# A spatial mix in seven half-size products instead of eight, in a fused attention and MLP kernel on one Trainium2 core

## The chip, the core and the metric

The kernel is one program on one core of a Trainium2 chip. The core has TensorE for matmuls (PE in the rows; PEld is its weight load), VectorE (DVE), ScalarE (ACT), GpSimd (POOL) and SyncE (SP, which here only issues transfers). Each engine works through its own instructions in order and waits on semaphores where it needs another's result. Matmul results land in PSUM, which TensorE writes and VectorE and ScalarE read; everything else lies in SBUF. The metric is the device time of one execution in microseconds (us). Lower is better.

## The reference, cut to what matters

Three parts follow one another: a hash-masked attention, a channel mix (`_moe_ref`) and a gated MLP with a mix along the sequence (`_moe2_ref`). The change lies in the last:

```python
def _moe2_ref(x, w_in, w_spatial, b_spatial, w_out):      # x (2, 768, 512)
    h = np.maximum(x @ w_in, 0.0)                         # (2, 768, 1024)
    u, v = (h[..., :512], h[..., 512:])
    mu = np.mean(v, axis=-1, keepdims=True)
    var = np.mean((v - mu) ** 2, axis=-1, keepdims=True)
    v_n = (v - mu) / np.sqrt(var + 1e-06)
    v_s = np.einsum('ts,bsd->btd', w_spatial, v_n) + b_spatial[None, :, None]
    gated = u * v_s
    return (gated @ w_out).astype(np.float32)
```

For each of the two batches the spatial mix is one product of a 768x768 matrix with a 768x512 matrix.

## The kernel before, in words

Every product is made three times at reduced precision to keep that of float32: each operand is held as a rounded high part and a remainder (low part), and `mm3` issues high by high, high by low and low by high (L178-184, so all its matmuls carry L183). A high part is a copy on ScalarE; the remainder is one subtraction of two SBUF tensors, on VectorE unless GpSimd is named (`split`, L129).

The order of the work is written out by hand. The steps are issued one after the other, and each ends with `tick()`, which issues the small jobs planned for that tick (`at_tick`, `later`). The last part has twelve token columns of 128 in three groups n of 512 tokens, and these steps:

- `step_u(n)`, four products of 12 matmuls: the half u of h, evacuated by a ReLU on ScalarE into XT (L772). It reads the group's input from `slots`, four tiles with high and low part; group 2 goes into the tiles that group 0 had, so `plan_split(2, ...)` fills them during the w steps (copy L650 on ScalarE, remainder L654 on VectorE).
- `step_w(n)`, four products of 12: the half v for 128 tokens each; here called a row. ReLU on ScalarE (L787), statistics and their aggregation on VectorE (L791, L792), then two ticks later a square root on ScalarE (L800), reciprocal and normalisation on VectorE (L801, L802), and a tick later the split into `vn`.
- `step_s(b, hf)`, four products of 18 matmuls with 384 columns: the spatial mix for one batch and one half of the output tokens. VectorE adds the bias (L826), multiplies with u (L828), and the result is split into a `parked` tile.
- `step_o(b, hf)`, three products of 12: the output product, copied by ScalarE (L851) and sent out by SP.

Their order is u0 u1 w0 w1 u2 w2, then s and o with the two batches interleaved. Transposed w_spatial is fetched by `plan_fetch` (once through SP, once rounded through GpSimd's queue) from tick 62 on, and its remainder is VectorE's (L757). The output weights' second half is prepared at ticks 78 and 81 by `plan_out`; the first row of w0 ends at tick 68, the last of w2 at 83. Products rotate through six PSUM banks (`bank`), so TensorE can be up to six products ahead of their readers.

Of the kernel before, what the change touches and what calls it, by code (L numbers as in the profile page):

```python
# [20 lines left out]
DM = 512  # L21
# [609 lines left out]
def mixers(tc, nc, mid, wide, top, XT, slots, parked, epsT, wr, wk, wv, w_in, w_spT, b_sp, w_out, out, split,  # L631
# [27 lines left out]
    with tc.tile_pool(name="m1", bufs=1) as m1:  # L659
# [62 lines left out]
        plan_out((2, 3), (78, 81))  # L722
# [14 lines left out]
    with tc.tile_pool(name="m2", bufs=1) as m2:  # L737
        vn, wsp = {}, []
        more = top.tile([128, 4, TB], F32, tag="x", name="more").bitcast(F32R).rearrange("p (m t) n -> p m t n", m=2)
        slots[6:] = [more[:, n] for n in range(2)]  # L740
# [3 lines left out]
        def plan_fetch(c, n):  # L744
            st = {}

            def load():
                t = mid.tile([128, 512, 2], U32, tag="w_raw", bufs=2, name="wst")
                st["t"] = t.rearrange("p a b -> p (a b)")[:, :S].bitcast(F32)
                nc.sync.dma_start(st["t"], w_spT[128 * c:128 * c + 128, :])  # L750
                if c % 3 == 0:
                    wsp.append(wide.tile([128, 2, 3, S], F32R, tag="PT", bufs=2, name="wsp"))
                nc.gpsimd.dma_start(wsp[c // 3][:, 0, c % 3, :], w_spT[128 * c:128 * c + 128, :])  # L753

            def rest():
                w = wsp[c // 3]
                nc.vector.tensor_sub(w[:, 1, c % 3, :], st["t"], w[:, 0, c % 3, :])  # L757

            at_tick(n, load)
            at_tick(n + 2, rest)  # L760
# [14 lines left out]
        def step_w(n):  # L775
            for j in range(4):
# [9 lines left out]
                t = m2.tile([128, DM], F32, tag="vt", bufs=4, name="vt")  # L786
# [6 lines left out]
                if n < 2:  # L793
                    tt = m2.tile([128, 2, DM], F32R, tag="vn", bufs=8, name="vn")
                else:
                    tt = wr[:, :, j, :]
                vn[divmod(4 * n + j, 6)] = tt

                def scale(t=t, mv=mv, sd=sd):
# [10 lines left out]
        def step_s(b, hf):  # L810
            t0 = hf * HS
            for m in range(4):
                o = bank("s")
                ms = slice(128 * m, 128 * m + 128)
                mm3(
                    o[:, :HS],
                    [
                        (
                            (vn[b, c][:, 0, ms], vn[b, c][:, 1, ms]),
                            (wsp[c // 3][:, 0, c % 3, t0:t0 + HS], wsp[c // 3][:, 1, c % 3, t0:t0 + HS]),  # L820
                        )
                        for c in range(6)
                    ],
                )
                f = mid.tile([128, HS], F32, tag="d", bufs=1, name="gs")
                nc.vector.tensor_add(f, o[:, :HS], bb[:, t0:t0 + HS])  # L826
                g = m2.tile([128, DM], F32, tag="vt", bufs=4, name="g")[:, :HS]
                nc.vector.tensor_mul(g, f, XT[:, m, b, t0:t0 + HS])  # L828
                t = parked[4 * hf + m]
                split(g, t[:, 0], t[:, 1])  # L830
                tick()

        def step_o(b, hf):
            for j in range(3):
# [5 lines left out]
                for cs in ((slice(0, 256), slice(256, DM)) if last else (slice(0, DM),)):  # L840
# [12 lines left out]
                    if last:  # L853
                        o = bank("o")
# [86 lines left out]
```

## Time and profile before

| | us |
|---|---|
| median of 3 runs (lowest, highest) | 532.88 (532.85, 533.25) |
| the profiled execution | 533.83 |
| its span, first to last instruction | 532.0 |

| engine | busy us | share of the span |
|---|---|---|
| TensorE | 526.0 | 99% |
| VectorE | 381.0 | 72% |
| ScalarE | 319.5 | 60% |
| GpSimd | 142.6 | 27% |

The rows below give a start in us from the span's start, a duration, the engine, the line of the program, the operation, what it writes and reads, and how many instructions were merged (x). Matmuls overlap, so their pace is read from start to start and not from a mean duration. In brackets stands the time the engine had been idle, and what ended it.

### The profile page before, as it was taken

What the parts mean: (1) busy time and instruction counts of PE and PEld (TensorE: products, weight loads), DVE (VectorE), ACT (ScalarE), POOL (GpSimd) and SP (SyncE); (2) the same over time, 40 slices, a digit from 0 to 9 for tenths busy, and PEclk for the clock granted to TensorE, in tenths of its full rate; (3) what the DMA queues carried; (4) which work ended last, traced back from release to release, by engine and by line L of the source; (5) the groups of instructions that cost most, each with busy time, mean ns of one, the idle gap of its engine ahead of it and who ended that gap; (6) DMA issues with size and microseconds to landing.
All of it is one profiled execution on the core that took longest, in us unless ns stands there. A gap on an engine that the chain in (4) does not pass through costs nothing.

```text
span 532.0 us, 8226 instructions
## 1 busy us (share of the span) xinstructions
PE 526.0 (99%) x2886; PEld 423.6 (80%) x2886; DVE 381.0 (72%) x794; ACT 319.5 (60%) x659; POOL 142.6 (27%) x157
## 2 busy tenths in 40 slices
PE   8999999999999999999999999999999999999997
PEld 6778676868687776688888888888888889989996
DVE  8787898888979789889777687345884948834230
ACT  8888788878888687566675557363433643221221
POOL 7859766776775441100000000001100000000000
PEclk9999999999999999999999999999999999999999
DMA  8985877687858310301221022005453100010102
GB/s 237 188 183 139 184 187 153 167 166 183 172 141 170 89 57 16 96 1 41 79 80 61 20 79 66 14 1 168 127 160 111 58 0 2 0 41 20 60 21 99
DMA packets 20041, 51.06 MB, mean 96 GB/s; under 512 B 3776, under 2 KB 6656, under 8 KB 20000
## 3 DMA queue, kind: packets, MB, share of 16 engines
q1 hardware_dynamic: 13424, 31.17, 19.7%
q0 software_dynamic: 6144, 19.07, 16.5%
q8 instruction: 23, 0.38, 0.3%
q10 hardware_dynamic: 432, 0.28, 0.2%
q14 instruction: 18, 0.15, 0.1%
HBM read 46.29 MB, written 3.19 MB: 93 GB/s over the span
## 4 chain that ended last, share of the span: by engine, by line
PE 93%; DMA 3%; DVE 1%; ACT 1%; SPq 0%; issue 0%; POOL 0%; POOLq 0%; DVEq 0%
PE o L183 14%; PE v L696 12%; PE o L461 11%; PE t L426 11%; PE s L394 11%; PE k L183 9%; PE s L183 7%; PE r L183 6%; PE w L183 6%; PE u L183 5%; DMA rb<-ds 1%; DMA w_raw<-in_w_r_dram 1%; PE z L292 1%; DVE p L404 1%; DMA ds<-rt 1%; PE o L284 1%
## 5 line engine op out<-in xcount | busy, mean ns | idle before, releaser
L404 DVE TENSOR_SCALAR_CACHE_REDUCE p<-s 128x768 f32<-128x768 f32 x96 | 91.3, 954 | 17.5 <-PE s L394 12.2
L416 ACT ACTIVATE p<-p,m 128x768 f32<-128x768 f32 x96 | 90.2, 941 | 13.2 <-DVE p L404 12.6
L394 PE MATMUL s<-tk 128*128 128x384 f32 x384 | 86.9, 356 | 0.0
L426 PEld LDWEIGHTS t<-ident,p 128*128 128x128 f32 x576 | 65.7, 140 | 20.2 <-issue 5.7
L426 PE MATMUL t<-ident,p 128*128 128x128 f32 x576 | 80.2, 276 | 0.9 <-ACT PT L432 0.7
L432 ACT COPY PT<-t 128x384 f32<-128x384 f32 x146 | 65.0, 477 | 22.0 <-PE t L426 21.8
L696 PE MATMUL v<-k,wv 128*128 128x512 f32 x288 | 68.8, 389 | 0.0
L461 PE MATMUL o<-PT,v 128*64 128x384 f32 x384 | 66.3, 491 | 0.6 <-DVE XT L473 0.6
L394 PEld LDWEIGHTS s<-tk 128*128 128x128 f32 x384 | 62.7, 189 | 2.6 <-POOL tk L359 0.7
L696 PEld LDWEIGHTS v<-k,wv 128*128 128x128 f32 x288 | 54.1, 188 | 11.2
L275 POOL TENSOR_TENSOR tk<-x,tk 64x384 fp32r<-64x384 f32 x56 | 58.1, 1057 | 10.6 <-DMA tk<-in_kq_dram 7.5
L461 PEld LDWEIGHTS o<-PT,v 128*64 128x64 f32 x384 | 25.8, 136 | 31.8 <-issue 30.2
L753 POOL DMA_DIRECT2D wsp<-in_w_spT_dram x6 | 3.3, 560 | 160.5 <-DVE w_a L45 145.9
L682 DVE TENSOR_TENSOR k<-kt,k 128x512 fp32r<-128x512 f32 x24 | 16.6, 690 | 30.2 <-ACT k L681 30.1
L183 PE MATMUL k<-tk,wk 128*128 128x512 f32 x144 | 35.6, 389 | 0.0
L183 PE MATMUL o<-wk,tk 128*128 128x512 f32 (+1 forms) x162 | 34.9, 374 | 0.0
L130 ACT CAST tk<-g 128x384 fp32r<-128x384 f32 x16 | 8.2, 513 | 42.0 <-DVE g L828 42.0
L183 PEld LDWEIGHTS o<-wk,tk 128*128 128x128 f32 x162 | 28.9, 188 | 5.3
L183 PEld LDWEIGHTS k<-tk,wk 128*128 128x128 f32 x144 | 27.0, 188 | 5.6
L156 DVE SCALAR_TENSOR_TENSOR f<-XT,msc,d 128x256 f32<-128x256 f32 x48 | 24.1, 503 | 6.5 <-ACT d L150 5.1
L183 PE MATMUL w<-wk,tk 128*128 128x512 f32 x114 | 26.5, 389 | 0.0
L432 DVE COPY PT<-t 128x384 f32<-128x384 f32 x46 | 24.8, 547 | 2.3 <-PE t L426 2.0
(131 smaller groups left out, 872.0 us busy)
## 6 DMA issues: line engine op xcount, KB each, us to landing
tk<-in_kq_dram POOLq DMA_DIRECT2D x30, 384.0 KB, 7.9
x<-in_kq_dram POOLq DMA_DIRECT2D x6, 768.0 KB, 5.4
w_raw<-in_w_k_dram SPq DMA_DIRECT2D x8, 512.0 KB
w_raw<-in_w_v_dram SPq DMA_DIRECT2D x8, 512.0 KB
w_raw<-in_w_in_dram SPq DMA_DIRECT2D x8, 512.0 KB
v<-in_vP_dram SPq DMA_DIRECT2D x8, 384.0 KB
rb<-ds SPq DMA_DIRECT2D x30, 96.0 KB
out_dram<-ot SPq DMA_DIRECT2D x11, 256.0 KB
```

Source lines behind the costliest of these rows:

```text
L130: nc.scalar.copy(hi, src)
L156: nc.vector.scalar_tensor_tensor(st["f"], x, mu, st["d"], op0=ALU.mult, op1=ALU.add)
L183: nc.tensor.matmul(o, a, x, start=(i == 0), stop=(i == len(seq) - 1))
L275: nc.gpsimd.tensor_sub(tk[l, 1 + 2 * t, o], raw[pp][l, t, o], tk[l, 2 * t, o])
L394: nc.tensor.matmul(s[:, c, :HS], w, t[:, n, c * HS:(c + 1) * HS], start=(n == 0), stop=(n == 1),)
L404: nc.vector.tensor_scalar(c, s[:, :, :HS], -0.125, BIG / 16, op0=ALU.mult, op1=ALU.min, accum_out=m)
L416: nc.scalar.activation(c, c, AF.Exp, bias=m, scale=-1.0, accum_out=den[g][:, u:u + 1])
L426: nc.tensor.transpose(t[:, 128 * n:128 * n + 128], p[:, k0:k0 + 128], ident)
L432: copy(PT[g][:, e, 3 * c:3 * c + 3, 128 * j:128 * j + 128], t[:, :HS].rearrange("p (n q) -> p n q", n=3),)
L461: nc.tensor.matmul(obank[64 * e:64 * e + 64, :HS], vt[g // 2][:, kt, e, :], PT[g][:, e, kt, :], start=(kt == 0), stop=(kt == 5),)
L682: held.append(lambda kk=k2[i]: nc.vector.tensor_sub(kk[:, 1], t, kk[:, 0]))
L696: nc.tensor.matmul(o, w, x, start=(c == 0 and k == 0), stop=(c == 7 and k == 2))
```

## The change

For each batch the 768x768 by 768x512 product is cut into quarters: a11, a12, a21, a22 of the normalised v (384 tokens by 256 channels, `raw`), and b11, b12, b21, b22 of transposed w_spatial (384 by 384). Four sums of the first and four of the second make seven products of quarter size in place of eight (the variant of Strassen's scheme with nested sums): a11 b11, a12 b21, s2 t2, s1 t1, s3 t3, a22 t4 and s4 b22. Each is done for two column blocks i of 128 channels, with 9 matmuls of 384 columns. VectorE adds each product from its PSUM bank into the outputs that need it (`pa`, `pb2`, `pu`).

- The sums of v and the parts of all seven operands are made on VectorE and ScalarE (`first_part` to `seventh_part`, planned at ticks 74 to 81 for batch 0, issued between the o steps for batch 1). They lie in tiles that other data has left: `more`, `wr`, `wk`, `parked`.
- The sums of w_spatial (L842-845, four subtractions of 384 columns) and their remainders (L856, two of 768) are made on GpSimd, for three blocks of 128 rows at ticks 68, 72 and 76, two ticks later for the remainders. b21 and b22 are loaded at ticks 79 and 82 (`plan_quarter`), into `wr` and `wk` once u2 and w2 are done with them.
- The normalisation follows its row after one tick instead of two and writes two tiles, so it becomes two instructions of 256 columns (L945). `vt` has two buffers instead of four.
- For i = 0 the remainder of a gated tile is GpSimd's, else VectorE's.
- The second half of the output weights is prepared at ticks 63 and 65; the s steps of a batch now both stand ahead of its o steps. The order of u and w steps is the same.

```diff
-        plan_out((2, 3), (78, 81))
+        plan_out((2, 3), (63, 65))
...
+        def s1_sum(b):
+            x = raw[b, "a22"]
+            nc.vector.tensor_add(x, raw[b, "a21"], x)
...
+            def plain_low():
+                nc.vector.tensor_sub(b11[c, 1], st[0][:, :HS], b11[c, 0])
+
+            def differences():
+                x, y = st[0], st[1]
+                nc.gpsimd.tensor_sub(x[:, :HS], x[:, HS:], x[:, :HS])
+                nc.gpsimd.tensor_sub(x[:, HS:], y[:, HS:], x[:, HS:])
+                nc.gpsimd.tensor_sub(y[:, HS:], y[:, HS:], x[:, :HS])
+                nc.gpsimd.tensor_sub(y[:, :HS], y[:, :HS], y[:, HS:])
...
+                for k in range(2):
+                    nc.scalar.copy(w22[k][:, 0, c], st[k])
+
+            def lows():
+                for k in range(2):
+                    nc.gpsimd.tensor_sub(w22[k][:, 1, c], st[k], w22[k][:, 0, c])
+
+            at_tick(n - 2, lambda: load(0))
+            at_tick(n - 2, lambda: load(1))
+            at_tick(n, plain_high)
+            at_tick(n, plain_low)
+            at_tick(n, differences)
+            at_tick(n + 2, highs)
+            at_tick(n + 2, lows)
...
+            def lows():
+                for c in range(3):
+                    k, o = divmod(c, 2)
+                    nc.vector.tensor_sub(home(1, c), st[k][:, HS * o:HS * o + HS], home(0, c))
...
-                    nc.vector.tensor_scalar(
-                        t, t, mv[:, 0:1], sd, op0=ALU.subtract, op1=ALU.mult
-                    )
-
-                later(2, scale)
-                later(3, lambda t=t, tt=tt: split(t, tt[:, 0], tt[:, 1]))
+                        nc.vector.tensor_scalar(
+                            raw[b, k][:, :, 128 * (c % 3):128 * (c % 3) + 128],
+                            t[:, 256 * h:256 * h + 256].rearrange("p (i n) -> p i n", i=2),
+                            mv[:, 0:1], sd, op0=ALU.subtract, op1=ALU.mult,
+                        )
+
+                later(1, scale)
...
+            o = product("a11", "b11")
+            nc.vector.tensor_add(pa, o, bias[0])
+            nc.vector.tensor_add(pb2, o, bias[1])
+            o = product("a12", "b21")
+            nc.vector.tensor_add(pu, o, pa)
+            gated(pu, i, 0)
+            o = product("s2", "t2")
+            nc.vector.tensor_add(pa, o, pa)
+            nc.vector.tensor_add(pb2, o, pb2)
+            middle()
+            o = product("s1", "t1")
+            nc.vector.tensor_add(pb2, o, pb2)
+            tick()
+            o = product("s3", "t3")
+            nc.vector.tensor_add(pu, o, pb2)
+            gated(pu, 2 + i, 1)
+            nc.vector.tensor_add(pa, o, pa)
+            o = product("a22", "t4")
+            nc.vector.tensor_add(pa, o, pa)
+            gated(pa, 2 + i, 0)
+            o = product("s4", "b22")
+            nc.vector.tensor_add(pb2, o, pb2)
+            gated(pb2, i, 1)
...
+        for c in range(3):
+            plan_spatial(c, (68, 72, 76)[c])
         plan_split(2, (71, 72, 73, 73))
+        h21, l21 = plan_quarter(lambda t, c: wr[:, t, c, :HS], 0, 79)
+        h22, l22 = plan_quarter(lambda t, c: wk[:, t, c, DM:DM + HS], HS, 82)
+        for n, job in zip(
+            (74, 75, 76, 77, 78, 80, 81),
+            (first_part, second_part, third_part, fourth_part, fifth_part, sixth_part, seventh_part),
+        ):
+            at_tick(n, lambda job=job: job(0))
+        at_tick(81, h21)
+        at_tick(82, l21)
...
-        step_s(0, 0)
-        step_s(0, 1)
-        step_o(0, 0)
+        step_s(0, 0, before_first, within_first)
+        step_s(0, 1, middle=lambda: low("s4", 0, 1))
...
+        step_o(0, 0, (lambda: first_part(1), lambda: second_part(1), lambda: third_part(1)))
+        step_o(0, 1, (more_sums, next_sums, last_sums))
         step_s(1, 0)
-        step_o(0, 1)
         step_s(1, 1)
         step_o(1, 0)
         step_o(1, 1)
```

First place: VectorE's order during the last rows of w1, up to the remainders that u2 needs (tk_0_84 and tk_1_85 are the tiles behind `slots`, vt a row after its ReLU, mv and sd its statistics). Before:

```order
L654 TENSOR_TENSOR tk_0_84<-XT,tk_0_84 128x512
L131 TENSOR_TENSOR vn<-vt,vn 128x512
L801 RECIPROCAL sd<-sd 128x1
L802 TENSOR_SCALAR vt<-vt,mv,sd 128x512
L791 BN_STATS st<-vt 128x6
L792 BN_AGGR mv<-st 128x2
L654 TENSOR_TENSOR tk_0_84<-XT,tk_0_84 128x512
L654 TENSOR_TENSOR tk_1_85<-XT,tk_1_85 128x512
```

The same stretch now:

```order
L838 TENSOR_TENSOR b_4600<-wst,b_4599 128x384
L654 TENSOR_TENSOR tk_0_84<-XT,tk_0_84 128x512
L941 RECIPROCAL sd<-sd 128x1
L945 TENSOR_SCALAR raw<-vt,mv,sd 128x2x128 x2
L931 BN_STATS st<-vt 128x6
L932 BN_AGGR mv<-st 128x2
L654 TENSOR_TENSOR tk_0_84<-XT,tk_0_84 128x512
L654 TENSOR_TENSOR tk_1_85<-XT,tk_1_85 128x512
```

The four remainders keep their place among the rows of w1; the normalisation between them is now that of the row just made, in two instructions, and a remainder of b11 (L838) has come in.

Second place: GpSimd's last instructions, as a difference (wst is a block of w_spatial as loaded, wsp its parts).

```order
 L77 TENSOR_TENSOR w_b<-w_b,wk 128x512
 L78 TENSOR_TENSOR wk<-w_b,w_a 128x512
-L753 DMA wsp<-in_w_spT_dram 128x768 x6
+L842 TENSOR_TENSOR wst<-wst 128x384
+L843 TENSOR_TENSOR wst<-wst 128x384
+L844 TENSOR_TENSOR wst<-wst 128x384
+L845 TENSOR_TENSOR wst<-wst 128x384
+L856 TENSOR_TENSOR wsp<-wst,wsp 128x768 x2
```

Six transfers are gone, and the six instructions shown with a + stand there three times, once for each block; eight splits of gated tiles follow.

Third place: VectorE's order during w2, from the sums of batch 0 to the remainders of b21 (wr<-wst). Before, three rows of w2 stand there with the split of their normalised values:

```order
L801 RECIPROCAL sd<-sd 128x1
L802 TENSOR_SCALAR vt<-vt,mv,sd 128x512
L791 BN_STATS st<-vt 128x6
L792 BN_AGGR mv<-st 128x2
L63 TENSOR_SCALAR w_p<-w_b 128x512
L66 SCALAR_TENSOR_TENSOR w_a<-w_raw,w_p 128x512
L131 TENSOR_TENSOR wr<-vt,wr 128x512
```

Now:

```order
L813 TENSOR_TENSOR raw<-raw 128x768
L798 TENSOR_TENSOR more<-raw,more 128x768
L809 TENSOR_TENSOR raw<-raw 128x768
L798 TENSOR_TENSOR v_a_4287<-raw,v_a_4287 128x768
L801 TENSOR_TENSOR tk_1_85<-raw,tk_1_85 128x384 x2
L817 TENSOR_TENSOR raw<-raw 128x768
L798 TENSOR_TENSOR v_a_4288<-raw,v_a_4288 128x768
L931 BN_STATS st<-vt 128x6
L932 BN_AGGR mv<-st 128x2
L801 TENSOR_TENSOR wr<-raw,wr 128x384
L886 TENSOR_TENSOR wr<-wst,wr 128x384 x3
```

The preparation of the output weights is gone from here, and the sums and remainders of the seven products stand ahead of w2's rows and of b21's remainders.

## Rows read from the trace of the kernel before

**Rows 1.** The page: busy time by engine, and the chain that ended last.

```profile
PE 526.0 (99%) x2886; PEld 423.6 (80%) x2886; DVE 381.0 (72%) x794; ACT 319.5 (60%) x659; POOL 142.6 (27%) x157
...
PE 93%; DMA 3%; DVE 1%; ACT 1%; SPq 0%; issue 0%; POOL 0%; POOLq 0%; DVEq 0%
```

**Rows 2.** Timeline of TensorE, last part: start, us, line, what, count.

```profile
402.08 12.40 PE L183 MATMUL w<-wk,tk 128*128 128x512 f32 x54
...
423.84 8.32 PE L183 MATMUL u<-tk,wr 128*128 128x512 f32 x36
...
445.61 3.29 PE L183 MATMUL s<-wsp,vn 128*128 128x384 f32 x18
...
470.58 8.37 PE L183 MATMUL o<-wk,tk 128*128 128x512 f32 x36
...
512.17 16.67 PE L183 MATMUL o<-wk,tk 128*128 128x512 f32 x84
```

**Rows 3.** TensorE's longest wait for another engine, whole span (total, times, longest).

```profile
PE o L284 <- POOL ident masks.py:199: 1.3, 1, 1.3
```

**Rows 4.** Span and granted clock.

```profile
core 0: 532.0 us, clock 1.000
```

**Rows 5.** Groups of instructions from 400 us on (busy us, mean ns), VectorE and ScalarE.

```profile
L130 ACT CAST tk<-g 128x384 fp32r<-128x384 f32 x16 | 8.2, 513 | 42.0 <-DVE g L828 42.0
...
L826 DVE TENSOR_TENSOR gs<-s,bb 128x384 f32<-128x384 f32 x12 | 6.7, 555 | 22.2 <-PE s L183 22.2
...
L802 DVE TENSOR_SCALAR vt<-vt,mv,sd 128x512 f32<-128x512 f32 x12 | 6.6, 546 | 0.4
...
L800 ACT ACTIVATE sd<-mv,epsT 128x1 f32<-128x1 f32 x12 | 3.5, 291 | 0.0
...
L801 DVE RECIPROCAL sd<-sd 128x1 f32<-128x1 f32 x12 | 1.9, 156 | 0.0
```

**Rows 6.** Timeline of VectorE, w0's first row and u2's last remainders.

```profile
405.63 0.69 DVE L791 BATCH_NORM_STATS2 st<-vt 128x6 f32<-128x512 f32 x1 [5.10 <-ACT vt L787]
...
406.46 0.94 DVE L757 TENSOR_TENSOR wsp<-wst,wsp 128x768 fp32r<-128x768 f32 x1
...
422.93 1.26 DVE L654 TENSOR_TENSOR tk<-XT,tk 128x512 fp32r<-128x512 f32 x2
```

**Rows 7.** Groups of instructions on GpSimd, whole span.

```profile
L77 POOL TENSOR_TENSOR w_b<-w_b,wk 128x512 f32<-128x512 f32 x8 | 10.2, 1280 | 13.8 <-ACT wk L72 13.5
...
L131 POOL TENSOR_TENSOR tk<-f,tk 128x256 fp32r<-128x256 f32 x8 | 5.8, 742 | 19.5 <-ACT tk L130 19.5
```

**Rows 8.** Timeline of GpSimd, three places in the attention.

```profile
68.06 5.59 POOL L275 TENSOR_TENSOR tk<-x,tk 64x384 fp32r<-64x384 f32 x5 [2.08 <-DMA tk<-in_kq_dram]
...
212.35 1.29 POOL L77 TENSOR_TENSOR w_b<-w_b,wk 128x512 f32<-128x512 f32 x1 [6.77 <-ACT wk L72]
217.34 1.30 POOL L78 TENSOR_TENSOR wk<-w_b,w_a 128x512 fp32r<-128x512 f32 x1 [3.70 <-DVE w_a L66]
```

**Rows 9.** Timeline of VectorE at the same three places.

```profile
68.55 0.80 DVE L63 TENSOR_SCALAR w_p<-w_b 128x512 uint32<-128x512 uint32 x1
69.38 1.37 DVE L66 SCALAR_TENSOR_TENSOR w_a<-w_raw,w_p 128x512 f32<-128x512 uint32 x1
...
212.48 0.55 DVE L473 TENSOR_TENSOR XT<-o,rb 128x384 f32<-128x384 f32 x1
...
215.21 0.48 DVE L156 SCALAR_TENSOR_TENSOR f<-XT,msc,d 128x256 f32<-128x256 f32 x1
...
216.51 0.68 DVE L66 SCALAR_TENSOR_TENSOR w_a<-w_raw,w_p 128x512 f32<-128x512 uint32 x1
217.11 0.35 DVE L152 TENSOR_SCALAR d<-XT,omu 128x256 f32<-128x256 f32 x1
217.50 1.42 DVE L156 SCALAR_TENSOR_TENSOR f<-XT,msc,d 128x256 f32<-128x256 f32 x1
218.84 0.41 DVE L50 TENSOR_SCALAR w_a<-w_a 128x512 uint32<-128x512 uint32 x1
```

More of the change, by code (lines that the diff above doesn't have):

```diff
@@ L737, in mixers @@
     with tc.tile_pool(name="m2", bufs=1) as m2:
-        vn, wsp = {}, []
-        more = top.tile([128, 4, TB], F32, tag="x", name="more").bitcast(F32R).rearrange("p (m t) n -> p m t n", m=2)
-        slots[6:] = [more[:, n] for n in range(2)]
+        spare = top.tile([128, 4, TB], F32, tag="x", name="more").bitcast(F32R)
+        pieces = spare.rearrange("p (m t) n -> p m t n", m=2)
+        slots[6:] = [pieces[:, n] for n in range(2)]
+        flat4 = spare.rearrange("p m n -> p (m n)")
+        one = flat4[:, :4 * HS].rearrange("p (t i n) -> p t i n", t=2, i=2)
@@ new lines, in op_of @@
+        def op_of(k, b, i):
+            if k in vop:
+                return vop[k][:, 0, i], vop[k][:, 1, i]
+            if k == "s1":
+                return one[:, 0, i], one[:, 1, i]
+            if k == "s2":
+                if b == 0:
+                    t = parked[6 + i]
+                elif i:
+                    t = parked[3]
+                else:
+                    t = work["s2"]
+                return t[:, 0], t[:, 1]
+            return wide_op(wr if k == "s3" else wk, i)
@@ new lines, in chunk, with like, both, high @@
+        def chunk(ap, c):
+            if len(ap.shape) == 3:
+                return ap[:, c]
+            return ap[:, 128 * c:128 * c + 128]
+        def like(ap, home):
+            if len(home.shape) == 3:
+                return ap.rearrange("p (c n) -> p c n", c=3)
+            return ap
+        def both(k):
+            t = one if k == "s1" else vop[k]
+            return t[:, 0], t[:, 1]
+        def high(k, b, i=None):
+            x = raw[b, {"s1": "a22", "s2": "a22", "s4": "a22", "s3": "a21"}.get(k, k)]
+            if i is None:
+                nc.scalar.copy(both(k)[0], x)
+            else:
+                hi = op_of(k, b, i)[0]
+                nc.scalar.copy(hi, like(x[:, i], hi))
@@ L755, in rest @@
[L755 to L760, printed above, removed]
+                for k in range(2):
+                    t = mid.tile([128, 512, 2], U32, tag="w_raw", bufs=2, name="wst")
+                    st[k] = t.rearrange("p a b -> p (a b)")[:, :2 * HS].bitcast(F32)
+                for c in range(3):
+                    k, o = divmod(c, 2)
+                    r = 128 * (c + 3)
+                    nc.sync.dma_start(st[k][:, HS * o:HS * o + HS], w_spT[r:r + 128, t0:t0 + HS])
@@ L792, in step_w @@
                 nc.vector.bn_aggr(mv, st)
[L793 to L799, printed above, removed]
+                b, c = divmod(4 * n + j, 6)
+                names = ("a12", "a22") if c > 2 else ("a11", "a21")
+                if b == 0 and c == 0:
+                    for k in ("a11", "a12", "a21", "a22"):
+                        raw[0, k] = raw_tile()
@@ new lines, in step_w, with step_s, product, gated @@
+                later(1, scale)
+                tick()
+        def step_s(b, i, early=lambda: None, middle=lambda: None):
+            pa, pb2, pu = work["a"], work["b"], work["u"]
+            def product(k, w):
+                o = bank("s")[:, :HS]
+                ah, al = op_of(k, b, i)
+                pairs = [((chunk(ah, c), chunk(al, c)), b_of(w, c)) for c in range(3)]
+                mm3(o, pairs)
+                return o
+            def gated(f, m, hf):
+                g = m2.tile([128, DM], F32, tag="vt", bufs=2, name="g")[:, :HS]
+                nc.vector.tensor_mul(g, f, XT[:, m, b, hf * HS:hf * HS + HS])
+                t = parked[4 * hf + m]
+                split(g, t[:, 0], t[:, 1], nc.gpsimd if not i else None)
+            early()
+            o = product("a11", "b11")
[21 more added lines that the diff above has]
+            gated(pb2, i, 1)
+            tick()
```

155 lines of the change are left out of this document (122 added, 33 removed).

## Prediction

> **What bounds the kernel now.** I read the page's busy table and its chain of waits first: TensorE is busy for 99% of the span, and the chain that ended last is 93% TensorE [rows 1]. So a matmul that goes is worth its pace, as long as nothing else becomes late, and an engine at 60 or 70% may become late in one stage. TensorE's timeline gives the paces from start to start: w0 and w1 are 96 matmuls of 512 columns between 402.08 and 423.84, 0.2267 us each; the first two s steps are 144 of 384 columns between 445.61 and 470.58, 0.1734 us each [rows 2]. Here TensorE never stands: its longest wait for an engine anywhere is 1.3 us, at the start, and its granted clock is 1.000, the 2.4 GHz level, throughout [rows 3, 4]. Last I looked at what the engines that must now do more have to spare, in VectorE's and GpSimd's timelines.
>
> **What the change saves.** Spatial matmuls before: 2 batches x 2 halves x 4 blocks x 18 = 288. After: 2 x 2 x 7 products x 9 = 252. 36 fewer, x 0.1734 = **6.24 us**. The shapes are the same, and so are the u, w and o steps. The profiled execution is 533.83 us with a span of 532.0, and lies 0.95 above the median of 532.88; I work out a difference and apply it to the median.
>
> **What it adds, and where that is hidden.** The transfers through GpSimd's queue go. The output weights' preparation moves from 433-454 to about 394-408, where VectorE is idle before (5.10 us ahead of 405.63 alone [rows 6]); only its last two subtractions, 1.3 us, are left behind the first row. Batch 1's sums, nine of 768 columns and six of 384 columns, some 11 us at 0.86 and 0.5 each, lie between o steps that take TensorE 72 x 0.2267 = 16.3 us; I cost them at nothing. Before, the o step behind an s step read tiles made one s step earlier; now it reads those just made, and waits for the last of them (fourth place). The rest falls between 405 and 480 us, on VectorE.
>
> **The port.** GpSimd now runs 3 blocks of 4 subtractions of 384 and 2 of 768 columns in that stretch. From 742 ns at 256 and 1280 at 512 columns [rows 7], 384 gives 1.01 and 768 some 1.82 (estimates from these two rows): 7.7 us a block. In the attention GpSimd's subtractions keep VectorE out: L156 took 1.42 us instead of 0.48 where it began at 217.50, and ended at 218.92, 0.28 after the subtraction that ran from 217.34 to 218.64; L66 took 1.37 instead of 0.68 between GpSimd's back-to-back ones, and the tensor-scalar L63, 0.80, where the like of it takes 0.41 [rows 8, 9]. An instruction of VectorE with one input in PSUM is not touched: L473 took 0.55 inside the one at 212.35 [rows 8, 9]. GpSimd loses too: five of them took 5.59 us around those. I read it as a port that one instruction holds to its end, and the other engine's next has it then; about 0.15 of an instruction's fixed time overlaps the wait. So VectorE's two-input and tensor-scalar instructions each wait for what is left of a GpSimd instruction, and GpSimd for theirs.
>
> The Trainium skill (GPSIMD Engine Reference, Key points) says the same of the kinds: GpSimd shares its SBUF interfaces with VectorE, in contention with instructions in a 2-port mode or with two SBUF inputs. It gives no size; the rows do, and by the rule all sums, remainders and normalising halves are of the kinds that wait, while the additions out of PSUM are not.
>
> **First place, u2.** Its third and fourth inputs' remainders (L654) ended at 424.2 before, just in time [rows 6]. u2 starts at 423.84 and needs the third after 7 matmuls, at 425.4. VectorE's own work from 405.63 to its end is now: 7 rows' statistics at 0.83 (405.63 to 406.46 [rows 6]) 5.8; the two late subtractions 1.3; two L838 1.0; three L654 at 0.6, 1.8; 6 reciprocals 1.0 [rows 5]; 12 normalising halves. No row shows a half; it costs between the 0.16 of a one-column instruction and the 0.546 of the whole [rows 5], and I take 0.30, near L152's 0.35 at the same 256 columns less overlap [rows 9]: 3.6. Sum 14.5. The square root now stands between statistics and normalisation of the same row, which leaves VectorE idle 0.3 to 0.45 (291 ns on ScalarE [rows 5]) three times, 1.2. Without the port the last row's ReLU, 6 x 2.72 us after 405.6, would set the end: 422.0 + 0.83 + 0.6 = 423.4. With it, followed instruction by instruction against GpSimd's (first block from 408.4, second from 420.5, once its rows have come), eight halves wait 0.4 to 1.6 us each, 6.0 in all, and the third remainder 0.8: 405.63 + 14.5 + 1.2 + 6.8 = **428.3**, 2.9 late. The fourth waits for a whole 768-column one, to 430.5, when TensorE, three matmuls on, wants it at 429.0: 1.5 more. TensorE stands **4.4**.
>
> **Second place, b21.** Product 2 needs its remainder (first of three L886). VectorE's work from 430.5: halves and reciprocals of four rows 3.1, statistics of four 3.3, seven 768-column sums and remainders ahead of b21 and one behind a dependency 7.0, five of 384 columns 2.5, the first L886 0.5: 16.4. It meets the third block's six subtractions: 0.8 three times, 0.75, 1.6, 1.55 = 6.3, and 0.7 of idle: 430.5 + 23.4 = **453.9**. TensorE, 4.4 late, asks for it at 445.61 + 4.4 + 10 x 0.1734 = 451.75: **2.1** more. (Unhindered it would have asked at 447.3.)
>
> **Third place, the seventh product.** It needs the remainder of s4, the last of the jobs put in the middle of step s. VectorE from 453.9: two L886, two rows' ends and one statistics 3.7, product 1 to 3's additions 2.7, b22 1.5, s4 0.5, and about 1 for GpSimd's first split: 463.7. TensorE, after product 2 at 455.2 and four more of 1.56, asks at 461.8: **1.9**.
>
> **Fourth place, the output.** VectorE then has 8 instructions of the first column block (4.5) and, in the second, 14 with three waits for ScalarE's cast (513 ns [rows 5]), 9.8, until parked tile 3 has its high part: 478.0. TensorE, 464.9 + 7 x 1.56 + 9 x 0.2267, asks at 477.9. I take **0.5**, between 0 and 1.
>
> Sum: 4.4 + 2.1 + 1.9 + 0.5 = 8.9 us of standing against 6.24 saved: **+2.7**, 536.5 for the profiled execution, **535.5** for the median. The places are not independent: VectorE is the bound from 408 to 478, so a smaller first wait is paid at the second. What can err is its time at the last places, by some 3 us either way: 532.5 to 539.
>
> **Rivals.**
> *The saving arrives* (VectorE and GpSimd pass each other by). For it: these instructions differ in kind from the attention's, and without port waits my sums end at 423.4, 446, 455 and 470, within 0.6 of what TensorE asks. Against it: rows 8 and 9. Then 6.24 less 0.6: 532.88 - 5.6 = 527.2, perhaps 526.5 to 529.
> *Only two-tensor instructions wait, not the normalising halves* (they take per-partition scalars, and no row shows such a one beside GpSimd). Takes away 6.0 at the first place; the sums of the second keep theirs. Standing of about 4 in all: 530.6, with 529 to 532.3.
> *The clock falls as well.* TensorE stands 2.9 us at once at u2, which happens nowhere before [rows 3]. If the granted clock then goes to the 1.2 GHz level for one product, 12 matmuls take 2.72 more; at two of the places 5.4, of which VectorE's lateness hides a part. Decided by whether the waits at u2 and b21 come in one piece. 538 to 541, say 540. The skill's page TensorE: Matmul & The Clock Gate (Part 1) has the clock fall when the engine idles; no row here shows it, as it never idles.
> *The change doesn't do what it says*: the order of u and w is as before, so that part has nothing to give; the 36 matmuls do go.
>
> **How the numbers follow.** Forecast 0.50 (of it 0.05 within 0.2%, the rest slower), saving arrives 0.25, halves don't wait 0.15 (0.11 faster, 0.04 same), clock 0.10. Under 0.2%, 1.07 us, is what a measurement of this kernel can't tell from no change. Faster 0.25 + 0.11 = 0.36, slower 0.45 + 0.10 = 0.55, same 0.09. The range, 526.8 to 540, leaves out the fastest end of the first rival and the end of the clock's; the forecast's own is 532.5 to 539.
>
> **What would show it.** Right: L945 and L654 of VectorE at 0.8 to 2 us while L842 to L856 run, and GpSimd's at over 1.2; TensorE idle at u2 behind VectorE's L654, at the second product behind L886, at the seventh behind L801; 252 matmuls in s at 0.173. Wrong: TensorE busy through u2 and the first s step with L945 at 0.35 throughout (the saving arrives), or idle behind ScalarE or a load of w_spatial, which I have as in time. If TensorE's clock reads under 1.00 after u2, the fourth case holds.

## The result, and the profile after

| | us |
|---|---|
| before, median of 9 runs beside it | 533.04 |
| changed kernel, median of 9 runs (lowest, highest) | 536.4 (535.77, 540.5) |
| ratio, 95% interval | 1.006 (1.0033 to 1.0086) |
| forecast | 535.5, range 526.8 to 540 |
| profiled execution, its span | 535.91, 534.1 |

The change makes the kernel 0.6% slower: the 36 matmuls go, and TensorE stands longer than they took. The busy table and the chain of the page after, to be read beside [rows 1]:

```profile
PE 522.6 (98%) x2850; PEld 418.5 (78%) x2850; DVE 417.7 (78%) x841; ACT 332.2 (62%) x682; POOL 177.0 (33%) x177
...
PE 78%; DVE 13%; DMA 4%; ACT 2%; issue 1%; SPq 0%; DVEq 0%; ACTq 0%
```

VectorE was 1% of the chain and is now 13% of it: that is how an engine that is busy for 78% of a span shows that it is the bound of one stage. Where, TensorE's waits from 375 us on tell (us in total, times, longest):

```profile
PE u L183 <- DVE tk L654: 4.1, 1, 4.1
PE s L183 <- DVE wk L801: 0.6, 1, 0.6
PE o L183 <- ACT tk L130: 0.5, 1, 0.5
```

And TensorE's timeline at these places, beside [rows 2]:

```profile
423.12 1.77 PE L183 MATMUL u<-tk,wr 128*128 128x512 f32 x7
428.99 9.68 PE L183 MATMUL u<-tk,wr 128*128 128x512 f32 x29 [4.11 <-DVE tk L654]
438.51 2.88 PE L183 MATMUL o<-tk,wr 128*128 128x512 f32 x12
...
453.70 1.72 PE L183 MATMUL o<-wr,v_a 128*128 128x384 f32 x9
...
461.50 0.51 PE L183 MATMUL s<-wk 128*128 128x384 f32 x2
462.62 1.50 PE L183 MATMUL s<-wk 128*128 128x384 f32 x7 [0.61 <-DVE wk L801]
...
474.91 2.25 PE L183 MATMUL o<-wk,tk 128*128 128x512 f32 x9
477.63 14.72 PE L183 MATMUL o<-wk,tk 128*128 128x512 f32 x63 [0.48 <-ACT tk L130]
...
514.10 16.71 PE L183 MATMUL o<-wk,tk 128*128 128x512 f32 x84
```

The part ahead of w0 ends up to some us earlier or later from execution to execution, in every kernel here (w0 starts at 401.36 here and at 402.08 before). So I compare **the stretch** from u2's start to the start of the last o step: 423.12 to 514.10, 90.98 us, against 423.84 to 512.17, 88.33, before [rows 2]: **+2.65**, where +2.66 was forecast. Each stretch, here and below, is read from one profiled execution. In it TensorE loses, by starts and paces:

- at u2 7 matmuls of 0.2267 end at 424.71, and it goes on at 428.99: 4.28 us in one piece;
- behind that stop 29 matmuls take 9.52 us (428.99 to 438.51) in place of 6.57: 2.95;
- at product 2 nothing; at the seventh product 462.62 - 461.50 - 2 x 0.1734 = 0.77; at the output 477.63 - 474.91 - 9 x 0.2267 = 0.68.

That is 8.68, and 2.44 above the 6.24 saved. The 0.21 that is left lies in the output step: its other 63 matmuls, from 477.63 to the next s step at 492.19, take 14.56, where the pace of before (36 between 470.58 and 478.78 [rows 2]) gives 14.35. The second item is TensorE's clock. The windows of the trace (stretch and length; busy time and count of PE, PEld, DVE, ACT, POOL; then granted clock, DMA share, GB/s):

```profile
423.84:440.00 16.16, 12.05 (x41) 9.38 (x40) 15.91 (x23) 9.54 (x17) 9.85 (x6) 0.79 0.16 49
440.00:456.00 16.00, 16.00 (x78) 13.89 (x77) 15.02 (x26) 6.70 (x16) 6.20 (x4) 1.00 0.21 61
```

0.79 is a mean over both levels: part of these 29 matmuls ran at 1.2 GHz, behind a stop of 4.28 us, and later ones at 2.4 again. (Read in windows of 2 us, the granted clock is 0.50 from 429 to 435 us and 1.00 from there on.) VectorE is busy for 15.91 of 16.16 us in the same window. Its own rows show with what, and GpSimd's beside them show why so long:

```profile
407.70 2.23 DVE L945 TENSOR_SCALAR raw<-vt,mv,sd 128x256 f32<-128x256 f32 x2
...
417.59 0.74 DVE L945 TENSOR_SCALAR raw<-vt,mv,sd 128x256 f32<-128x256 f32 x2
...
422.26 0.68 DVE L931 BATCH_NORM_STATS2 st<-vt 128x6 f32<-128x512 f32 x1
...
423.94 2.78 DVE L945 TENSOR_SCALAR raw<-vt,mv,sd 128x256 f32<-128x256 f32 x2
...
427.46 2.08 DVE L654 TENSOR_TENSOR tk<-XT,tk 128x512 fp32r<-128x512 f32 x2
...
435.14 0.95 DVE L798 TENSOR_TENSOR more<-raw,more 128x768 fp32r<-128x768 f32 x1
...
444.50 2.60 DVE L798 TENSOR_TENSOR v_a<-raw,v_a 128x768 fp32r<-128x768 f32 x1
...
452.53 1.46 DVE L886 TENSOR_TENSOR wr<-wst,wr 128x384 fp32r<-128x384 f32 x3
...
459.80 2.30 DVE L886 TENSOR_TENSOR wk<-wst,wk 128x384 fp32r<-128x384 f32 x3
```

```profile
407.67 1.02 POOL L842 TENSOR_TENSOR wst<-wst 128x384 f32<-128x384 f32 x1 [189.74 <-DVE sd L941]
...
422.26 1.02 POOL L844 TENSOR_TENSOR wst<-wst 128x384 f32<-128x384 f32 x1
...
424.77 3.62 POOL L856 TENSOR_TENSOR wsp<-wst,wsp 128x768 fp32r<-128x768 f32 x2
...
434.49 2.48 POOL L842 TENSOR_TENSOR wst<-wst 128x384 f32<-128x384 f32 x1 [6.09 <-DVE more L838]
...
441.60 4.68 POOL L856 TENSOR_TENSOR wsp<-wst,wsp 128x768 fp32r<-128x768 f32 x2
```

A pair of halves takes 0.74 us where GpSimd is idle (417.59) and up to 2.78 beside it; the same remainder L798 takes 0.95 and 2.60. Summed over the five pairs, L654 and the six sums and remainders that run beside GpSimd, VectorE loses 6.85 + 1.0 + 6.3 = 14.2 us. GpSimd's own instructions stretch too, from 1.02 to 2.48 and from 3.62 to 4.68. Not all of VectorE's work on SBUF waits: the statistics, with one input, keep their 0.68 us inside GpSimd's L844 (both start at 422.26).

### The profile page after: what moved, and what is told of

The parts are those of the page before. It is cut to its first block, busy times and chain, and to the rows that moved or that the text cites. A ratio compares the mean times of both kernels' runs of the same rounds, so it can differ in the third digit from the quotient of the medians.

```text
span 534.1 us, 8304 instructions
## 1 busy us (share of the span) xinstructions
PE 522.6 (98%) x2850; PEld 418.5 (78%) x2850; DVE 417.7 (78%) x841; ACT 332.2 (62%) x682; POOL 177.0 (33%) x177
## 3 DMA queue, kind: packets, MB, share of 16 engines
HBM read 45.11 MB, written 3.19 MB: 90 GB/s over the span
## 4 chain that ended last, share of the span: by engine, by line
PE 78%; DVE 13%; DMA 4%; ACT 2%; issue 1%; SPq 0%; DVEq 0%; ACTq 0%
PE v L696 12%; PE o L461 11%; PE o L183 11%; PE t L426 11%; PE s L394 10%; PE k L183 9%; PE r L183 6%; PE s L183 4%; PE u L183 3%; DVE raw L945 3%; DVE st L931 1%; DMA rb<-ds 1%; DMA w_raw<-in_w_r_dram 1%; DVE v_a L798 1%; DMA x<-in_kq_dram 1%
## 5 line engine op out<-in xcount | busy, mean ns | idle before, releaser
L842 POOL TENSOR_TENSOR wst<-wst 128x384 f32<-128x384 f32 x3 | 4.9, 1618 | 199.5 <-DVE sd L941 189.7
L275 POOL TENSOR_TENSOR tk<-x,tk 64x384 fp32r<-64x384 f32 x56 | 59.2, 1078 | 8.3 <-DMA tk<-in_kq_dram 6.4
L183 PE MATMUL u<-tk,wr 128*128 128x512 f32 x90 | 24.3, 428 | 4.1 <-DVE tk L654 4.1
```

The lines of the kernel that those rows point to most:

```text
L183: nc.tensor.matmul(o, a, x, start=(i == 0), stop=(i == len(seq) - 1))
L275: nc.gpsimd.tensor_sub(tk[l, 1 + 2 * t, o], raw[pp][l, t, o], tk[l, 2 * t, o])
```

## The experiments

Ratios are to the kernel before, in runs on the same chip; on that scale the changed kernel is 1.006.

| run | median us | ratio, 95% interval | stretch us |
|---|---|---|---|
| changed kernel | 536.4 | 1.006 (1.0033 to 1.0086) | 90.98 |
| e1, no work for GpSimd | 529.01 | 0.9893 (0.9838 to 0.9949) | 82.37 |
| e2, earlier split | 538.37 | 1.0091 (1.0054 to 1.0129) | 92.36 |
| e3, halves on ScalarE | 536.6 | 1.0022 (0.9981 to 1.0063) | 89.19 |
| e4, TensorE kept busy | 536.68 | 1.003 (0.9992 to 1.0069) | 90.91 |
| e5, sums on VectorE | 535.07 | 1.0026 (1.0007 to 1.0044) | 90.14 |
| e7, as e5, earlier split | 535.55 | 1.004 (1.0016 to 1.0063) | 90.60 |
| e6b, results unread | 539.46 | 1.0098 (1.0068 to 1.0129) | 92.63 |
| e8b, one-input copies | 528.79 | 0.9896 (0.9863 to 0.9929) | 82.59 |
| e9, sums made earlier | 530.54 | 0.992 (0.9889 to 0.995) | 84.46 |
| e10, as e9, b22 on GpSimd | 529.8 | 0.9912 (0.9883 to 0.9942) | 83.40 |

**e1: is it GpSimd's work?**

```diff
-            at_tick(n, differences)
+            if c == 0:
+                at_tick(61, cleared)
...
-            at_tick(n + 2, lows)
```

> Left out: GpSimd's sums and remainders of w_spatial (L842-845, L856), so the parts of t1 to t4 are those of plain quarters with remainders of zero. GpSimd is then idle between 400 us and its first split of a gated tile. Port theory (VectorE waits for the port that GpSimd holds, and is the bound from 408 to 478 us): each pair of normalising halves takes 0.74 us instead of 1.1 to 2.8, u2's third remainder is done about 423 to 424, TensorE does not stop at u2, its clock stays at 1.00, what remains is up to 1 us at the seventh product and the output: about 527.5 us, 5 to 6 faster than before, some 8 to 9 faster than the changed kernel. Rival (VectorE's own order is too long, with the square root standing between a row's statistics and its halves; the port matters little): the stop at u2 keeps most of its 4.3 us and the time stays at 534 to 536.

TensorE waits for nothing after 375 us, and the stretch is 82.37: 5.96 shorter than before, of 6.24 saved. VectorE's rows are short again:

```profile
422.79 1.26 DVE L654 TENSOR_TENSOR tk<-XT,tk 128x512 fp32r<-128x512 f32 x2
...
436.15 0.95 DVE L798 TENSOR_TENSOR v_a<-raw,v_a 128x768 fp32r<-128x768 f32 x1
```

So the saving is real, and all of the loss hangs on GpSimd's 18 instructions. Whether by the port, as the prediction has it, or because someone waits for their results, this run doesn't say.

**e6, e6b: port or results?** The first try (e6) wrote GpSimd's results into `parked[0]`, which lies in the memory of the w steps' inputs:

```diff
+            free = parked[0].rearrange("p t n -> p (t n)")
...
+                        nc.gpsimd.tensor_sub(free[:, :HS], st[k][:, HS:], st[k][:, :HS])
```

> GpSimd does its subtractions at the same ticks, of the same sizes and on the same inputs as in the changed kernel, but writes them to a tile that nobody reads (it leaves out the sums and remainders of w_spatial, as in the run without GpSimd's work, so the output is another). My theory, the shared port: nobody waits for a result of GpSimd's, yet VectorE's pairs of halves take 1.1 us or more beside it and the sums 1.6 us or more, TensorE stands 2 us or more at u2 behind L654, the stretch from u2's start to the last o step is 89 to 92 us, and the time 534 to 538 us. Rival, what was lost is waiting for GpSimd's results (sums, remainders): then TensorE does not stand, the stretch is 82 to 84 us as without the work, and the time 527 to 530 us.

It took 555.49 us, and TensorE waited for GpSimd at five places (up to 5.3 us): a false dependence that I had built in, which says nothing of the port. In e6b the results stay in the staging tiles, and the high parts are copied ahead of them:

```diff
-                    nc.gpsimd.tensor_sub(w22[k][:, 1, c], st[k], w22[k][:, 0, c])
...
+                    nc.gpsimd.tensor_sub(st[k], st[k], w22[k][:, 0, c])
...
+            at_tick(n, highs)
...
-            at_tick(n + 2, highs)
```

> The run before this with unread results wrote them into a tile that shares its memory with the inputs of the w steps, so that TensorE waited for GpSimd; here they stay in the staging tiles. GpSimd does its eighteen subtractions at the same ticks, of the same sizes; the high parts are copied ahead of them (two ticks earlier than in the changed kernel), so no engine reads a result of GpSimd's (left out: the sums of w_spatial and the remainders of t1 to t4). My theory, the shared port: VectorE's halves and sums still stretch beside GpSimd (pairs of halves over 1.1 us against 0.74, sums over 1.6 against 0.95), TensorE stands over 2 us at u2 or later behind VectorE, the stretch from u2's start to the last o step is 88 to 92 us (90.98 in the changed kernel, 82.37 without GpSimd's work), and the time 533 to 538 us. Rival, what was lost is waiting for GpSimd's results: no stand, 82 to 84 us, 527 to 530 us.

Not the results: nobody reads what GpSimd makes, and the stands are those of the changed kernel and a little more, since ScalarE's copies, which now come ahead of the square roots, delay a row. (e8b below has the same early copies and hardly stands, so they are not the cause.) GpSimd's running is enough to hold VectorE up. TensorE's row at u2 and VectorE's behind it:

```profile
430.61 8.20 PE L183 MATMUL u<-tk,wr 128*128 128x512 f32 x29 [4.08 <-DVE tk L654]
```

```profile
425.62 3.53 DVE L949 TENSOR_SCALAR raw<-vt,mv,sd 128x256 f32<-128x256 f32 x2
```

**e8, e8b: must GpSimd's instruction have two inputs?** The subtractions of e6 and e6b became copies; e8 has e6's false dependence (543.56 us).

```diff
-                nc.gpsimd.tensor_sub(x[:, :HS], x[:, HS:], x[:, :HS])
+                nc.gpsimd.tensor_copy(x[:, :HS], x[:, HS:])
...
-                    nc.gpsimd.tensor_sub(st[k], st[k], w22[k][:, 0, c])
+                    nc.gpsimd.tensor_copy(st[k], w22[k][:, 0, c])
```

> As the run in which GpSimd's results go unused, with each of GpSimd's subtractions made a copy of the same number of columns, which has one input in place of two. Theory, only GpSimd's two-input instructions keep VectorE out: halves at 0.74 us a pair, sums at 0.95, no stand at u2, stretch 82 to 84 us, 527 to 530 us. Rival, any work of GpSimd's on SBUF holds the port: as with the subtractions, scaled by the duration of the copies; stretch over 86 us, 531 us or more.

> As the run beside it with unread results, each subtraction of GpSimd's made a copy of as many columns, with one input. In the earlier run with copies VectorE's two L654 took 2.52 us beside two 768-column copies, and a pair of halves 1.14, so I expect that copies hold VectorE up too, for as long as they last, which is about half (0.54 at 384, 0.9 to 1.0 at 768 columns against 1.02 and 1.85): stretch from u2's start to the last o step 83.5 to 88 us, and 528 to 533 us. Rival, only instructions of GpSimd's with two inputs hold the port: every pair of halves 0.74, every sum 0.95, stretch 82 to 83.5 us.

In e8b GpSimd's copies take half as long (0.51 us at 384 columns, where the subtraction took 1.02), and VectorE still waits for them:

```profile
409.51 0.51 POOL L854 COPY wst<-wst 128x384 f32<-128x384 f32 x1
...
411.10 1.60 POOL L860 COPY wst<-wsp 128x768 f32<-128x768 f32 x2
```

```profile
412.12 1.05 DVE L949 TENSOR_SCALAR raw<-vt,mv,sd 128x256 f32<-128x256 f32 x2
...
438.36 1.57 DVE L798 TENSOR_TENSOR v_a<-raw,v_a 128x768 fp32r<-128x768 f32 x1
```

So one input is enough to hold VectorE up (1.05 for 0.74, 1.57 for 0.95). The stretch, 82.59, came out below my 83.5 to 88 and inside the rival's 82 to 83.5; but the rival had every pair of halves at 0.74 and every sum at 0.95, and four pairs take 0.93 to 1.08 and the four sums of 768 columns beside the last block 1.14 to 1.57. VectorE has room for such waits, here some 3.7 us, before TensorE feels more than 0.23 at the output. My theory of the mechanism holds, my sum for it was too high.

**e2: does VectorE bound the whole stretch?** The remainders of u2's inputs move ahead of block 2's worst part.

```diff
-        plan_split(2, (71, 72, 73, 73))
+        plan_split(2, (71, 71, 72, 72))
```

> Whole computation. The last group's inputs are split one tick earlier (71, 71, 72, 72), so that their remainders stand on VectorE ahead of the normalising halves of two rows that they waited behind. Theory that VectorE is the bound as far as the output: the stop at u2 (4.3 us of standing and some 3 of slow clock) goes, but b21's remainder and s4's come no earlier, so TensorE stands 4 to 6 us at the second and seventh product instead, and the time is 534.5 to 536.5. Rival (the stop at u2 is the loss by itself): 7 us faster than the changed kernel, about 529.

```profile
427.44 6.86 PE L183 MATMUL u<-tk,wr 128*128 128x512 f32 x29 [0.44 <-DVE tk L654]
...
452.68 0.69 PE L183 MATMUL o<-wr,v_a 128*128 128x384 f32 x1 [3.19 <-ACT wr L881]
456.60 2.93 PE L183 MATMUL o<-wr,v_a 128*128 128x384 f32 x8 [3.23 <-DVE wr L886]
```

u2's stop shrinks from 4.1 to 0.44 and comes back at product 2 as 3.19 and 3.23, with slow matmuls behind it. The place moved, the sum didn't fall; it is 1.4 longer, and the time lies above the 534.5 to 536.5 that I expected. The trace shows where VectorE lost more:

```profile
430.40 2.31 ACT L789 CAST v_a<-raw 128x768 fp32r<-128x768 f32 x3 [1.42 <-DVE raw L945]
```

```profile
432.94 0.16 DVE L941 RECIPROCAL sd<-sd 128x1 f32<-128x1 f32 x1 [1.75 <-ACT sd L940]
```

With the L654 gone from that place, VectorE idles 1.75 us for a square root that stands on ScalarE behind three casts; in the changed kernel the two L654 filled that time. Its first L886 then starts 30.77 us after u2's start, and not 29.41: 1.36 later. ScalarE's copy of b21 (the 3.19) is no other cause: it stands behind a square root that had waited 3.65 us for VectorE's statistics.

**e4: what does the clock's fall cost?** Twenty matmuls whose result is overwritten fill u2's stop.

```diff
+                if n == 2 and m == 0:
+                    for _ in range(20):
+                        nc.tensor.matmul(o, wr[:, 0, 0, :128], wr[:, 0, 1, :], start=True, stop=True)
```

> Whole computation, and 20 matmuls of 512 columns more ahead of u2's first product, into the bank that it then starts anew: TensorE is busy (4.5 us) where it stood. Its granted clock should then stay at 1.00 through u2, which gives 29 matmuls back their 0.2267 us (2.9 us). Theory that VectorE is the bound as far as the output: TensorE comes earlier to b21 and waits there instead, 535.5 to 536.5 as the changed kernel. Rival (the clock's fall is a part of the sum): 533 to 534.

```profile
435.76 8.36 PE L183 MATMUL u<-tk,wr 128*128 128x512 f32 x36
...
461.30 2.29 PE L183 MATMUL o<-wr,v_a 128*128 128x384 f32 x8 [1.83 <-DVE wr L886]
```

Now u2 runs at full pace, and TensorE stands at product 2, where the forecast had it: the stretch, from the fillers' start at 431.23, is 90.91, as without them. In this execution the clock falls behind product 2's stand instead (0.73 from 461.3 to 463 us and 0.58 to 466), so the profile alone would not tell what the fall costs. The times do: four of the eleven executions show a granted clock of 1.000 over the whole and took 536.17 to 538.64 us, the five at 0.996 and 0.997 took 536.22 to 540.45. (The profiled one, at 0.991, took 543.95, but lost its time ahead of u2.) Of the changed kernel's nine, four at 0.993 took 535.77 to 537.11 and four at 0.997 took 535.86 to 537.15. So the 2.95 us that the clock took at u2 were hidden in VectorE's lateness.

**e3: are the normalising halves the culprit?** ScalarE makes them, a tick later.

```diff
+                    nc.vector.scalar_tensor_tensor(nb, mv[:, 0:1], -1.0, sd, op0=ALU.mult, op1=ALU.mult)
...
-                        nc.vector.tensor_scalar(
+                        nc.scalar.activation(
...
-                            mv[:, 0:1], sd, op0=ALU.subtract, op1=ALU.mult,
+                            AF.Identity, bias=nb, scale=sd,
```

> Whole computation. The 24 normalising halves move from VectorE to ScalarE (scale and bias by row, with one more one-column instruction on VectorE for the bias), one tick later than now. By the port theory halves account for 8 of the 9 waits ahead of u2: its third remainder is done about 424, no stop there, and b21's remainder about 446: 527.5 to 530. Rival (waits are for ScalarE's queue and GpSimd's results, not for the port): ScalarE gets 24 instructions of about 0.4 us more in that stretch, evacuates later, and the time is 535 or more.

A miss, by 6.6 us from the near end of the range. Taking 24 halves from VectorE left the stands at u2 (2.83 and 1.27 us):

```profile
417.22 0.16 DVE L942 RECIPROCAL sd<-sd 128x1 f32<-128x1 f32 x1 [2.34 <-ACT sd L941]
417.42 1.35 DVE L943 SCALAR_TENSOR_TENSOR nb<-mv,sd 128x1 f32<-128x1 f32 x1
...
427.69 0.69 DVE L932 BATCH_NORM_STATS2 st<-vt 128x6 f32<-128x512 f32 x1 [1.71 <-ACT vt L927]
428.41 0.18 DVE L933 BATCH_NORM_AGGREGATE mv<-st 128x2 f32<-128x6 f32 x1
428.51 4.53 DVE L654 TENSOR_TENSOR tk<-XT,tk 128x512 fp32r<-128x512 f32 x2
```

```profile
415.11 3.65 POOL L856 TENSOR_TENSOR wsp<-wst,wsp 128x768 fp32r<-128x768 f32 x2
```

The halves now stand in ScalarE's queue ahead of the ReLUs, so the last row came 1.71 us late; then the two L654 began just behind GpSimd's 768-column remainders (from 428.45, 4.05 us for two) and took 4.53 for 1.26. Even `nb`, of one column and with two inputs in SBUF, takes 1.35 beside GpSimd and 0.16 alone (420.31), and it ends at 418.77, as GpSimd's pair does at 418.76: the wait is what is left of GpSimd's instruction, whatever VectorE's size. The reciprocal ahead of it, of one column and one input, keeps its 0.16 beside the same pair.

**e5, e7: the same work on VectorE.**

```diff
-                nc.gpsimd.tensor_sub(x[:, :HS], x[:, HS:], x[:, :HS])
+                nc.vector.tensor_sub(x[:, :HS], x[:, HS:], x[:, :HS])
...
-                    nc.gpsimd.tensor_sub(w22[k][:, 1, c], st[k], w22[k][:, 0, c])
+                    nc.vector.tensor_sub(w22[k][:, 1, c], st[k], w22[k][:, 0, c])
```

> The twelve sums of w_spatial and the six remainders of 768 columns that GpSimd made (L842-845, L856) are VectorE's instead; nothing else is changed. VectorE gets 12 x 0.51 + 6 x 0.95 = 11.8 us of work more. My theory: GpSimd's instructions cost VectorE about as much in waiting for the shared port (in the changed kernel's trace some 4.4 us over the six pairs of halves, 0.8 at L654, 5.5 over six sums under GpSimd, and a few more: 11 to 14), so with GpSimd idle each of VectorE's two-input instructions is back at its own duration (pair of halves 0.74, sum 0.95), TensorE still stands at u2 by 2 to 5 us, and from u2's start to the last o step it takes 88.5 to 92.5 us (90.98 in the changed kernel): 534 to 538 us. Rival, GpSimd takes real work off VectorE: then most of the 11.8 us shows, 98 us or more for that stretch and 541 us or more.

> As the run with the sums and remainders of w_spatial on VectorE, and the remainders of u2's inputs planned one tick earlier for three of four (ticks 71, 71, 72, 72), so that they stand ahead of the second block's two remainders of 768 columns. VectorE's work up to the third L654 is then shorter by 1.9 us or more: TensorE stands 0 to 2 us at u2, and VectorE, which remains the bound, makes TensorE stand at product 2 or later instead. Theory: stretch from u2's start to the last o step 87.5 to 91.5 us, 533 to 537 us, within 1.5 of the run without the earlier split. Rival, the first stand is what costs: 2 us or more faster than that run, 531 to 534 us.

With all 18 on VectorE, some 12 us more for it, the stretch is 90.14, 0.84 shorter than with GpSimd's help. So GpSimd took nothing off VectorE: its help was paid back in waits. e7 repeats e2 without GpSimd's 18: u2's stop shrinks (to 0.7), and product 2's comes (0.9 and 3.5 us). The rival, that the first stand is what costs, falls again.

**e9, e10: the work where VectorE has time.** The sums are made in the key and value steps, sent to DRAM and loaded back; the remainders stay with VectorE as in e7. e10 gives b22's remainders to GpSimd.

```diff
+        sums = [dram.tile([128, S], F32, tag=f"sum{r}", bufs=1, name="sums") for r in range(6)]
...
+        for i, n in enumerate((21, 23, 39, 40, 43, 50)):
+            plan_sums(i // 2, i % 2, n)
...
-                nc.sync.dma_start(st[k], w_spT[128 * r:128 * r + 128, :])
+                nc.sync.dma_start(st[k], sums[c + 3 * k])
...
+            l22(nc.gpsimd)
```

(The last line is e10's.)

> The sums of w_spatial leave the crowded stretch: VectorE makes them during the key and value steps (six half blocks of 4 x 192 columns at ticks 23 to 52, where it is busy 50 to 80% of the time), SyncE stores them to DRAM and the spatial stage loads them back at ticks 66 to 74; b11 comes by a load of its own. The remainders of 768 columns are VectorE's, with the split of u2's inputs ahead of the second block's (as in the run on VectorE with the early split); GpSimd does nothing there. VectorE has 12 x 0.51 = 6.1 us less than in that run between 405 and 478 us (stretch 90.6). My theory, VectorE is the bound of that stretch: stands at u2 and product 2 fall from 4.4 to 0 to 1.5 us, stretch 84 to 87 us, 528 to 532 us, faster than both kernels. Rival, the stands come from the order of the pieces and not from the sum of VectorE's work: stretch 88 us or more, 533 us or more; or the loads back come late and TensorE or ScalarE wait for them.

> As the run with the sums made earlier, and b22's three remainders of 384 columns given from VectorE (three in 2.31 us) to GpSimd, in the stretch in which VectorE mostly adds products out of PSUM. Theory: an instruction with an input in PSUM does not wait for the port, so the additions stay at 0.55 us beside GpSimd; VectorE has 2.3 us less in front of s4's remainder and loses up to 1 us of it at the multiplications with u and at that remainder, which read SBUF. GpSimd needs 3 x 1.02 us from the casts' end on (452.57 to 454.07 in that run), so they are ready 0 to 0.6 us after TensorE asks (456.5). The third stand falls from 1.4 to 0.2 to 0.8 us, stretch from u2's start to the last o step 83.3 to 84.2 us (84.46 in that run), 529.3 to 530.4 us. Rival, the additions out of PSUM are held up too: over 0.8 us each beside GpSimd, and no gain, 84.4 us or more.

e9 beats both kernels: 0.8% faster than before. TensorE's rows of e9:

```profile
424.88 8.32 PE L183 MATMUL u<-tk,wr 128*128 128x512 f32 x36
...
457.87 1.50 PE L183 MATMUL s<-wk 128*128 128x384 f32 x7 [1.25 <-DVE wk L832]
...
472.88 14.71 PE L183 MATMUL o<-wk,tk 128*128 128x512 f32 x63 [0.48 <-ACT tk L130]
...
509.34 16.70 PE L183 MATMUL o<-wk,tk 128*128 128x512 f32 x84
```

u2 doesn't stop; of the stands the seventh product's and the output's are left. e10 cuts the first of these from 1.41 to 0.45 us, as forecast (stretch 83.40), though its time, 529.8, is not told apart from e9's by these intervals. Its rows, GpSimd's and VectorE's:

```profile
457.07 3.28 POOL L913 TENSOR_TENSOR wk<-wst,wk 128x384 fp32r<-128x384 f32 x3 [234.19 <-ACT wk L908]
```

```profile
458.43 0.55 DVE L1004 TENSOR_TENSOR raw<-s,raw 128x384 f32<-128x384 f32 x1
458.90 0.54 DVE L1005 TENSOR_TENSOR raw<-s,raw 128x384 f32<-128x384 f32 x1
459.37 1.40 DVE L832 TENSOR_TENSOR wk<-raw,wk 128x384 fp32r<-128x384 f32 x1
```

Beside GpSimd, additions out of PSUM keep their 0.55 us, and the remainder that reads SBUF twice goes from 0.55 to 1.40.

## Why the prediction was right, step by step

The forecast's times are on the scale of the kernel before, where w0 and u2 start 0.72 us later than in the profiled execution of the changed kernel; so I add 0.72 to what that trace shows before comparing.

- **The saving, 6.24**: right; e1 and e8b show 5.96 and 5.74 of it when TensorE hardly stands.
- **The port**: right in what it does, and now shown by itself (e1, e6b, and in e3 `nb`, which waits to the end of GpSimd's instruction); that it is a port is a name for this, which no run here can show. The halves wait too, so the rival that spared them falls. The half itself is 0.37 (0.74 a pair), not the 0.30 chosen; it lay within the bounds. The halves' waits ahead of u2 are 6.85 for the 6.0 reckoned.
- **First place, 4.4**: 4.28, but in one piece and not in two. The third remainder ended at about 429.6 (forecast 428.3, though the terms given for it add up to 428.1) and the fourth at 430.3 (430.5), so the fourth cost nothing.
- **Second place, 2.1**: measured 0, the step that failed. VectorE was there at about 453.8, as forecast (453.9); but TensorE asked at 454.6 and not at 451.75. The forecast had put its pace behind u2's stop at the full clock, and the slower clock cost 2.95. The rival "the clock falls as well" thus came true in its mechanism (2.72 reckoned for one product), and not in its time: the sentence that "a smaller first wait is paid at the second" holds the other way round as well, and e4 shows the second place at 1.83 as soon as the clock stays up through u2.
- **Third and fourth place, 1.9 and 0.5**: 0.77 and 0.68. At s4's remainder VectorE was done at 463.3. The prediction writes 463.7, but its own terms (453.9 and 9.4) add up to 463.3: 0.4 of the 1.9 is a slip in the sum. The rest is TensorE, which asked at 462.6 and not at 461.8. The wait for GpSimd's first split, put at about 1, came: b22's three L886 take 2.30 us beside it, and b21's three 1.46.
- **The sum**: +2.7 forecast, +2.65 in the stretch. That the two agree to 0.01 is luck: the slip of 0.4 makes up for the output, which cost 0.68 and the 0.21 behind it in place of 0.5. What made the sum robust was the bound that lies behind all four places: TensorE may lose its time at u2, in its clock or at product 2, and arrives when VectorE does. The first L886 starts 29.41 us after u2's start in the changed kernel, and 1.36 later than that in e2, 1.66 later in e6b, 0.08 later in e4 and 0.85 earlier in e5; the stretches differ by 1.38, 1.65, -0.07 and -0.84. e2, e4 and e7 moved the stand from place to place without a gain; only less work or less waiting for VectorE (e1, e8b, e9) moved the end by much.
- **The Trainium skill's rule** (GPSIMD Engine Reference, Key points) is that GpSimd contends with VectorE's instructions of two SBUF inputs or in a 2-port mode. The runs agree for two SBUF inputs, and the tensor-scalar halves wait as well (0.74 to 2.78 a pair); which mode those run in no trace here shows. On GpSimd's side the rule asks nothing, and e8b agrees that a copy with one input is enough.

## What to carry to other kernels

Here GpSimd relieved VectorE only while VectorE read PSUM, made statistics or idled; beside VectorE's sums, remainders and halves on SBUF, an instruction given to it cost about what it took off (14.2 us of waits for 12 us of work). Where one engine is late at several places in a row, sum its work over the stretch: a stand that goes at the first place can come back at the next, and a slower clock costs nothing as long as the lateness behind it is another engine's. (In e2 and e7 no stand follows product 2, so what the slow matmuls there cost is not shown.) Before such a trade of matmuls for sums, look for an earlier stage with room, even by way of DRAM (e9).

## What was not expected of the hardware

- A one-column instruction of VectorE's with two SBUF inputs waits as a wide one does: 1.35 us beside GpSimd, 0.16 alone (e3). Statistics and reciprocals, with one input, don't wait: 0.68 and 0.16 either way.
- GpSimd's copies, with one input, hold VectorE up as its subtractions do, but for half the time: 0.51 and 1.02 us at 384 columns.
- Keeping TensorE at 2.4 GHz through u2's stop was worth nothing here: 90.91 us against 90.98 (e4).
- Taking two remainders out of VectorE's way made the stretch longer (e2): they had filled a wait for ScalarE, which then came to light, 1.75 us.
- Still open: e7's first L886 starts 0.59 us earlier than the changed kernel's, and its stretch is only 0.38 shorter; e3's starts 0.81 earlier, and its stretch is 1.79 shorter, of which 0.81 goes to b22's L886 (1.49 for 2.30).
